# One group's sums of x made a stage earlier, two GpSimd sums put behind a quad, and the last rows stored in halves, in a fused windowed-attention and GEGLU kernel

## The chip, the cores and the metric

The kernel runs on one core of a Trainium2 chip. The core has five engines, each with its own queue of instructions: TensorE (PE in the profile; its weight loads are PEld), VectorE (DVE), ScalarE (ACT), GpSimd (POOL, here "Pool") and SyncE (SP), which here only issues transfers and passes semaphores on. The metric is the device time of one execution in microseconds, taken as the median of several runs.

## The reference

Eight batches of eight heads, 576 positions and head size 64 go through causal attention with a window of 128 and a linear (ALiBi) penalty; the result, 4608 tokens by 512, goes through a gated feed-forward block with an exact GELU.

```python
scores = scale * np.matmul(q, k.transpose(0, 1, 3, 2))
mask = (rel >= 0) & (rel < window)
scores = np.where(mask, scores + bias[None], -1000000000.0)
attn = np.exp(scores - max); attn = attn / (sum(attn) + 1e-09)
x = np.matmul(attn, v)             # as 4608 tokens x 512
...
g = x @ w_gate                     # 512 -> 1536
gelu = 0.5 * g * (1.0 + erf(g * inv_sqrt2))
return gelu * (x @ w_val) @ w_out  # 1536 -> 512
```

## The kernel before, in words

Attention works on batches of 576 tokens, the feed-forward block on nine groups (0 to 8) of 512 tokens. The attention result is kept transposed in `xT`, a ring of 2048 token columns. Group 7 holds tokens 3584 to 4095: its first 448 come from batch 6, its last 64 from batch 7, the last batch. The order of all instructions is written out by hand, and the work of a coming batch is put between the products of the running group. Each engine takes its own instructions strictly in order, so an instruction that waits holds up all behind it on that engine.

**Gate blocks.** `gate_val(g, f)` makes 128 of the 1536 hidden features: eight matmuls into two PSUM banks (L650), a GELU on ScalarE (L657) and the product of the two halves on VectorE into `hT` (L658). A group has twelve of them, f = 0 to 11. In groups 7 and 8, `gate_quad` makes f = 0 to 3 and f = 6 to 9 as two quads, each with seven block products in place of eight (L810). For that it needs sums and differences of parts of x (`combine_x`, VectorE, L785, kept in `T`) and of the gate and value weights (`combine_weights`, Pool, L768). A quad ends with products into `hT`: two on VectorE (L852), two on Pool (L853).

**Output products.** From group 2 on, the output projection is done in the same way: seven products P(1) to P(7) for each of two column halves a = 0 and 1, six matmuls of 256 columns each (L753). Their left sides need sums of parts of `hT`: `combine_left(g, lo, hi, which)` makes, for pairs lo to hi of feature blocks, s1 (which = 0), s2 (1), s4 (2) in `left` and the difference a21 (3) in place in `hT` (L728). Most are on VectorE; in groups 7 and 8 those of pairs 0 and 1, which come from the first quad, are on Pool. `gather_out` empties the PSUM banks: copies p1, u2, p5 and c21 on ScalarE (L866, L868, L872, L876), additions c11, c22 and c12 on VectorE (L870, L874, L879). Of a row block's two output tiles `hi` is finished by c21 and `lo` by c12; `finished` notes a store of 128 rows by 512 columns, which `store()` issues on SP (L677).

**Around the change.** In group 6 the output products of a = 0 are mixed with `values` of batch 7 (L504): products of probabilities and v into six PSUM banks, scaled by VectorE into `xT` (L579) with reciprocals that came by a transfer. P(1) of a = 1 uses the bank of the first of those six, so it waits until `scale[0]` and `scale[1]` have read it. Ahead of these two on VectorE stood c22 and then the four operations of `combine_x(g + 1, 0, 192)`. This call needs only tokens of batch 6; the rest, `combine_x(g + 1, 192, 256)`, needs batch 7 and stands at the group's end. On Pool, eight weight sums for the first quad are made in group 6 in two fours; a small copy to `mark` (L1270) ahead of each four holds Pool until the named VectorE result is there, and another mark (L1243) ahead of the second quad's sums waits for the last `combine_x`.

Of the kernel before, what the change touches and what calls it, by code (L numbers as in the profile page):

```python
# [36 lines left out]
def kernel(  # L37
# [10 lines left out]
    nc = tc.nc  # L48
    B, H, S, D = q.shape
# [4 lines left out]
    NG = NTOK // 512  # L54
# [618 lines left out]
    done, stores = [0], []  # L673
# [107 lines left out]
    def combine_x(g, lo=0, hi=256):  # L781
        b11, b12, b21, b22, t1, t2, t3, t4 = (t[:, :, lo:hi] for t in tokens(g) + sums_x(g))
        for to, a, b, op in ((t1, b12, b11, ALU.subtract), (t2, b22, t1, ALU.subtract),
                             (t3, b22, b12, ALU.subtract), (t4, b21, t2, ALU.subtract)):
            nc.vector.tensor_tensor(out=to, in0=a, in1=b, op=op)  # L785
# [66 lines left out]
            nc.vector.tensor_tensor(out=hidden(u, 0), in0=both(banks["x", u]), in1=both(gelus[u]), op=ALU.mult)  # L852
            nc.gpsimd.tensor_tensor(out=hidden(u, 1), in0=both(P5[u]), in1=both(gelus[2 + u]), op=ALU.mult)  # L853

    def finished(g, t, osb):
        r0 = 512 * g + 128 * t
        stores.append(dict(out=out[r0:r0 + 128, :], in_=osb))

    def gather_out(g, a, what, copy=nc.scalar.copy):
        x, y, z = (made.get((g, a, n)) for n in "xyz")  # L860
        if what == "p1":
            made[g, a, "lo"] = o_pool.tile([128, DM], FP32, name="osb")
            made[g, a, "hi"] = o_pool.tile([128, DM], FP32, name="osb")
        lo, hi = made[g, a, "lo"], made[g, a, "hi"]
        if what == "p1":
            copy(out=lo[:, 0:256], in_=x)  # L866
        elif what == "u2":
            copy(out=lo[:, 256:512], in_=x)  # L868
        elif what == "c11":
            nc.vector.tensor_tensor(out=lo[:, 0:256], in0=z, in1=lo[:, 0:256], op=ALU.add)  # L870
        elif what == "p5":
            copy(out=hi[:, 256:512], in_=y)  # L872
        elif what == "c22":
            nc.vector.tensor_tensor(out=hi[:, 256:512], in0=x, in1=hi[:, 256:512], op=ALU.add)  # L874
        elif what == "c21":
            copy(out=hi[:, 0:256], in_=x)  # L876
            finished(g, 2 + a, hi)
        elif what == "c12":
            nc.vector.tensor_tensor(out=lo[:, 256:512], in0=y, in1=lo[:, 256:512], op=ALU.add)  # L879
            finished(g, a, lo)  # L880

    def out_last(g):
        last = o_pool.tile([128, DM], FP32, name="osb")
# [233 lines left out]
    def out_products(g):  # L1117
        b = g + 2
        O = lambda what, a, copy=act: gather_out(g, a, what, copy)
        P = lambda n, a: product(g, n, a)  # L1120
        if b > B:
            for n, after in ((1, ("p1",)), (2, ()), (6, ("u2", "c11")), (5, ("p5",)), (7, ("c22",)), (4, ("c21",)),
                             (3, ("c12",))):
                for a in (0, 1):
                    P(n, a)
                    for what in after:
                        O(what, a)
                store()
                if n == 6 and g + 1 < NG:
                    combine_x(g + 1)  # L1130
            return
        P(1, 0)
        P(2, 0)
        O("p1", 0)
        urgent = 512 * (g + 2) - S * (b - 1)
        if b == B:
            P(6, 0)
            O("u2", 0)
            O("c11", 0)
            P(5, 0)  # L1140
            O("p5", 0)
            P(7, 0)
            O("c22", 0)
            combine_x(g + 1, 0, 192)
            scale = values(b - 1, later=True)
            P(4, 0)
            O("c21", 0)
            P(3, 0)
            scale[0]()
            scale[1]()  # L1150
            O("c12", 0)
            P(1, 1)
            O("p1", 1)
            store()
            P(2, 1)
            for do in scale[2:]:
                do()
            O("c11", 1)
            P(6, 1)
            O("u2", 1)  # L1160
            P(5, 1)
            O("p5", 1)
            P(7, 1)
            O("c22", 1)
            P(3, 1)
            O("c12", 1)
            P(4, 1)
            O("c21", 1)
            combine_x(g + 1, 192, 256)
            return  # L1170
        exp_table()
        O("c11", 0)
        later = []
        scores2(b, 0, later)
        A = later[0]
        P(6, 0)
        O("u2", 0, dve)
        P(5, 0)
        for n in (0, 1, 3):
            A[n]()  # L1180
        O("p5", 0)
        A[2]()
        P(7, 0)
        O("c22", 0)
        A[4]()
        for n in (5, 6, 7):
            A[n]()
        P(1, 1)
        P(4, 0)
        P(3, 0)  # L1190
        O("p1", 1)
        O("c21", 0)
        O("c12", 0)
        A[8]()
        A[9]()
        scores2(b, 2, later)
        A = later[1]
        P(2, 1)
        P(6, 1)
        O("u2", 1, dve)  # L1200
        O("c11", 1)
        add(b, 0, None, (0,))
        P(5, 1)
        for n in (0, 1, 3, 5):
            A[n]()
        O("p5", 1)
        A[2]()
        P(7, 1)
        O("c22", 1)
        A[4]()  # L1210
        for n in (6, 7):
            A[n]()
        store()
        scale, more = values(b - 1, urgent=urgent)
        for do in scale:
            do()
        P(4, 1)
        P(3, 1)
        O("c21", 1)
        for do in more:  # L1220
            do()
        O("c12", 1)
        A[8]()
        A[9]()
        add(b, 0, None, (2, 1))
        put_off.append(lambda: add(b, 2))
# [3 lines left out]
    for g in range(NG):  # L1230
# [7 lines left out]
        if g >= B - 1:  # L1238
            for f in range(NF):
                if f in QUADS:  # L1240
                    if g == B - 1 and f == 0:
                        sums = combine_weights(6)
                        nc.gpsimd.tensor_copy(out=mark, in_=sums_x(g)[3][0:1, 1, 254:256])  # L1243
                        for do in sums[:4]:
                            do()
                    gate_quad(g, f)
                    if g == B - 1 and f == 0:
                        for do in sums[4:]:
                            do()
                elif not any(f0 < f < f0 + 4 for f0 in QUADS):  # L1250
                    gate_val(g, f)
                if f == 4:
                    store()
                if f == 5:
                    combine_left(g, 0, 2, engine=nc.gpsimd)
                if f == 6:
                    combine_left(g, 2, 3, (0, 1))
            for which in ((0, 1), (3,), (2,)):
                for lo, hi in ((3, 5), (5, 6)) if 0 in which else ((2, 5), (5, 6)):
                    combine_left(g, lo, hi, which)  # L1260
            out_products(g)
            continue
        for f in range(9 if g == 0 else 0, NF):
            gate_val(g, f)
            if g == B - 2 and f in (2, NF - 1):
                if f == 2:
                    sums = combine_weights(0)
                else:
                    combine_left(g, 5, 6)
                nc.gpsimd.tensor_copy(out=mark, in_=hid[g][0:1, f, 510:512] if f == 2 else left[0:1, 2, 5, 0:2])  # L1270
                for do in (sums[:4] if f == 2 else sums[4:]):
                    do()
            if f == 1:
                for do in put_off:
                    do()
                put_off.clear()
                store()
            if g == 1 and f in (3, 5, 7, 9):
                combine_right(f // 2 - 1)
            if g in PRODUCTS and f in ((7, 9) if g == B - 2 else (7, 9, 11)):  # L1280
                combine_left(g, *{7: (0, 3), 9: (3, 5), 11: (5, 6)}[f])
            if g == 2 and f == 2:
                add(3, 2, act, (1,))
            if g == 0 and f == 10:
                masks_of_last_blocks(0, 8)
            if g == 0 and f == 9:
                for c in range(4):
                    for w in (0, 1):
                        transpose(1, w, c, (act, dve)[w])
            if 2 <= g < B - 1:  # L1290
                if f == (5 if g == 2 else 4):
                    sums4(g + 1)
                if f == (7 if g == 2 else 6):
                    gather(g + 1)
                if f == (9 if g == 2 else 8):
                    spread_dma(g + 1)
                if f == 9 and g + 2 < B:

                    nc.gpsimd.tensor_copy(out=mark, in_=hid[g][0:1, f, 0:2])  # L1299
                    if g + 3 < B:  # L1300
                        load_qk(g + 3)
                    load_v(g + 2)
# [47 lines left out]
```

## Time and profile before

| What | Value |
|---|---|
| median of 3 runs | 332.83 us (332.52 to 333.11) |
| the profiled execution: its own time | 334.23 us |
| its span, first to last instruction | 332.4 us |
| PE busy | 322.2 us, 97% |
| DVE busy | 257.0 us, 77% |
| ACT busy | 186.1 us, 56% |
| POOL busy | 145.8 us, 44% |
| granted TensorE clock | 1.0 over the span |

A row of a timeline has the start in microseconds of the span, the time from the start of the first to the end of the last instruction of the row, the engine, the line in the kernel, the operation, written tile, read tile, shapes and the number of instructions; in square brackets stands how long the engine was idle ahead of it and what ended that. A queue's own work (issuing a transfer) has a q behind the engine's name. A PE row with many matmuls lists starts and ends of a pipeline: one matmul of 256 columns takes about 0.27 us by itself and 0.11 us in a run of them.

### The profile page before, as it was taken

How to read it: one execution, taken by the hardware profiler on the slowest of the kernel's cores; microseconds unless marked ns; L12 is line 12 of the kernel's file. 1: busy time of each engine (PE TensorE's matmuls, PEld its weight loads, DVE VectorE, ACT ScalarE, POOL GpSimd, SP SyncE). 2: the span in 40 equal slices, each digit the busy share in tenths (PEclk: the TensorE clock that was granted, in tenths of full speed). 3: DMA queues.
4: the chain of work that ended last, by engine and by line, in shares of the span. 5: the costliest groups of instructions: out<-in, count | busy, mean ns of one | idle time of the engine just before them, and what ended most of it. 6: DMA issues, size and time to landing. Idle time of an engine off the chain costs nothing. (4 is left out here: it accounts for less than half of the span.)

```text
span 332.4 us, 9100 instructions
## 1 busy us (share of the span) xinstructions
PE 322.2 (97%) x3640; PEld 201.8 (61%) x3640; DVE 257.0 (77%) x529; ACT 186.1 (56%) x365; POOL 145.8 (44%) x179
## 2 busy tenths in 40 slices
PE   8999998999999999999999999999999899999995
PEld 6566654544554468445854585448644687788774
DVE  7788776365679967978798969976998876876692
ACT  7974686536798356434843384239533237636641
POOL 5974689280095085006900490032032528910720
PEclk9999999999999999999999999999999999999999
DMA  8999999999699999969994799559204230003003
GB/s 213 167 196 190 203 169 183 148 202 151 145 116 158 144 155 190 197 130 178 191 154 127 152 173 195 128 131 129 85 1 103 66 108 0 2 0 128 3 0 126
DMA packets 149630, 43.54 MB, mean 131 GB/s; under 512 B 133556, under 2 KB 142420, under 8 KB 149588
## 3 DMA queue, kind: packets, MB, share of 16 engines
q0 software_dynamic: 107456, 18.10, 72.4%
q1 hardware_dynamic: 38960, 18.69, 26.6%
q10 hardware_dynamic: 3172, 6.19, 8.2%
q8 instruction: 28, 0.46, 0.6%
q14 instruction: 14, 0.11, 0.1%
HBM read 43.65 MB, written 9.53 MB: 160 GB/s over the span
## 5 line engine op out<-in xcount | busy, mean ns | idle before, releaser
L657 ACT ACTIVATE gelu<-ps 128x512 bf16<-128x512 f32 (+3 forms) x101 | 55.9, 559 | 85.8 <-PE ps L650 78.2
L650 PE MATMUL ps<-xT,wg 128*128 128x512 bf16 (+4 forms) x408 | 96.4, 358 | 0.1
L650 PE MATMUL ps<-xT,wv 128*128 128x512 bf16 (+4 forms) x408 | 96.3, 358 | 0.0
L658 DVE TENSOR_TENSOR hT<-ps,gelu 128x512 bf16<-128x512 f32 (+3 forms) x101 | 62.0, 636 | 26.8 <-PE ps L650 19.0
L650 PEld LDWEIGHTS <-wv 128*128 128x128 bf16 x408 | 38.7, 98 | 41.2 <-DVE xT L558 0.5
L650 PEld LDWEIGHTS <-wg 128*128 128x128 bf16 x408 | 38.0, 98 | 38.7 <-issue 0.4
L234 ACT ACTIVATE P<-ps 128x512 bf16<-128x512 f32 (+1 forms) x108 | 52.4, 578 | 4.2 <-PE ps L303 2.1
L237 DVE TENSOR_TENSOR P<-P,emask 128x768 bf16<-128x768 bf16 x60 | 32.0, 554 | 8.1 <-ACT P L234 6.3
L753 PEld LDWEIGHTS <-hT 128*128 128x128 bf16 x336 | 31.8, 97 | 10.0 <-DVE xT L579 2.0
L117 POOL DMA_DIRECT2D vb<-in_v_dram x40 | 34.0, 893 | 3.9 <-DMA ks<-in_k_dram 1.2
L1299 POOL COPY mark<-hT 1x2 bf16<-1x2 bf16 x4 | 1.5, 366 | 74.1 <-DVE hT L658 74.1
L117 POOL DMA_DIRECT2D ks<-in_k_dram x30 | 25.4, 887 | 3.8 <-DMA qs<-in_q_dram 3.5
L753 PEld LDWEIGHTS <-left 128*128 128x128 bf16 x252 | 24.3, 98 | 3.0
L117 POOL DMA_DIRECT2D qs<-in_q_dram x30 | 25.1, 855 | 1.8 <-issue 0.9
L753 PE MATMUL ps<-wo,hT 128*128 128x256 bf16 x168 | 21.4, 273 | 2.8 <-DVE xT L579 1.7
L753 PE MATMUL ps<-right,hT 128*128 128x256 bf16 x168 | 22.1, 272 | 0.0
L753 PE MATMUL ps<-right,left 128*128 128x256 bf16 x168 | 20.3, 273 | 0.0
L504 PE MATMUL ps<-P,vb 64*64 64x192 bf16 (+2 forms) x752 | 18.3, 221 | 0.8 <-ACT P L234 0.7
L687 PE MATMUL ps<-wo,hT 128*128 128x512 bf16 x72 | 17.1, 380 | 1.1 <-issue 1.1
L853 POOL TENSOR_TENSOR hT<-qT,qs 128x512 bf16<-128x512 f32 x8 | 9.2, 1173 | 19.2 <-ACT qs L821 19.2
L504 PEld LDWEIGHTS <-vb 64*64 64x64 bf16 x752 | 15.0, 107 | 3.6 <-issue 2.7
L818 DVE TENSOR_TENSOR qT<-ps,qT 128x512 f32<-128x512 f32 x16 | 10.3, 686 | 8.5 <-PE ps L810 8.5
(141 smaller groups left out, 448.0 us busy)
## 6 DMA issues: line engine op xcount, KB each, us to landing
out_dram<-osb SPq DMA_DIRECT2D x36, 256.0 KB
rb<-rd ACTq DMA_DIRECT2D x10, 576.0 KB
vb<-in_v_dram POOLq DMA_DIRECT2D x32, 128.0 KB, 6.6
qs<-in_q_dram POOLq DMA_DIRECT2D x24, 128.0 KB, 5.8
ks<-in_k_dram POOLq DMA_DIRECT2D x24, 128.0 KB, 8.3
wo<-in_moe_w_out_dram POOLq DMA_DIRECT2D x4, 384.0 KB, 12.1
wg<-in_moe_w_gate_dram POOLq DMA_DIRECT2D x5, 256.0 KB, 8.4
wv<-in_moe_w_val_dram POOLq DMA_DIRECT2D x5, 256.0 KB, 8.9
```

The source lines that it names most:

```text
L117: nc.gpsimd.dma_start(out=t[at:at + n, j, :].rearrange("p (h d) -> p h d", h=H), in_=src[b][:, 128 * j:128 * j + n, :].rearrange("h p d -> ...
L234: nc.scalar.activation(out=dst, in_=src, func=AF.Exp, scale=0.125)
L237: nc.vector.tensor_tensor(out=dst, in0=dst, in1=m, op=ALU.mult)
L504: mm = nc.tensor.matmul(out=out, lhsT=lhsT, rhs=prob(b)[half, c, i, col:col + q1 - q0], start=all(t[2] != u for t in todo[:n]), stop=True, ...
L650: nc.tensor.matmul(out=ps[:, a:e], lhsT=w[:, c, 128 * f:128 * (f + 1)], rhs=xT[:, c, t0 + lo + a:t0 + lo + e], start=begins and a == 0, st ...
L657: nc.scalar.activation(out=gl[:, 0:n], in_=pg, func=AF.Gelu)
L658: nc.vector.tensor_tensor(out=hid[g][:, f, lo:hi], in0=pv, in1=gl[:, 0:n], op=ALU.mult)
L687: nc.tensor.matmul(out=acc[g], lhsT=hid[g][:, f, 128 * t:128 * (t + 1)], rhs=wo[:, f, :], start=(f == 0), stop=(f == NF - 1))
L753: nc.tensor.matmul(out=made[g, a, into], lhsT=lhsT, rhs=rhs, start=first and i == 0, stop=i == NF // 2 - 1, skip_group_check=True)
L818: nc.vector.tensor_tensor(out=to[u], in0=banks[n, u], in1=to[u], op=ALU.add)
L853: nc.gpsimd.tensor_tensor(out=hidden(u, 1), in0=both(P5[u]), in1=both(gelus[2 + u]), op=ALU.mult)
L1299: nc.gpsimd.tensor_copy(out=mark, in_=hid[g][0:1, f, 0:2])
```

## The change

Three edits, none of which changes an arithmetic operation.

1. `combine_x(g + 1, 0, 192)` leaves the output products of group 6 and is made in that group's gate blocks, behind block f = 6.
2. In groups 7 and 8, Pool makes only s1 and s2 of pairs 0 and 1 ahead of the second quad's products into `hT`; a21 and s4 of these pairs come behind them, a21 first.
3. In group 8 the `lo` tiles are stored in two halves of 256 columns: the first half once c11 has made it, the second behind c12. The second half of a = 1 is issued by ScalarE's queue, the rest by SP.

```diff
-    def finished(g, t, osb):
+    def finished(g, t, osb, cols=slice(0, 512), queue=None):
...
+        args = dict(out=out[r0:r0 + 128, cols], in_=osb[:, cols])
+        if queue is None:
+            stores.append(args)
+        else:
+            queue.dma_start(**args)
...
         elif what == "c11":
             nc.vector.tensor_tensor(out=lo[:, 0:256], in0=z, in1=lo[:, 0:256], op=ALU.add)
+            if g == NG - 1:
+                finished(g, a, lo, slice(0, 256))
...
-            finished(g, a, lo)
+            finished(g, a, lo, slice(256 if g == NG - 1 else 0, 512), nc.scalar if g == NG - 1 and a else None)
...
             O("c22", 0)
-            combine_x(g + 1, 0, 192)
             scale = values(b - 1, later=True)
...
                 if f == 5:
-                    combine_left(g, 0, 2, engine=nc.gpsimd)
+                    combine_left(g, 0, 2, (0, 1), engine=nc.gpsimd)
                 if f == 6:
                     combine_left(g, 2, 3, (0, 1))
+                    combine_left(g, 0, 2, (3, 2), engine=nc.gpsimd)
...
             gate_val(g, f)
+            if g == B - 2 and f == 6:
+                combine_x(g + 1, 0, 192)
```

VectorE's queue before, from the end of group 6's gate blocks into its output products; `osb` is an output tile, `T` holds the sums of x, `rb` the reciprocals:

```order
L728 TENSOR_TENSOR hT<-hT 128x256
L870 TENSOR_TENSOR osb<-ps,osb 128x256
L874 TENSOR_TENSOR osb<-ps,osb 128x256
L785 TENSOR_TENSOR T<-xT 128x2x192
L785 TENSOR_TENSOR T<-xT,T 128x2x192
L785 TENSOR_TENSOR T<-xT 128x2x192
L785 TENSOR_TENSOR T<-xT,T 128x2x192
L579 TENSOR_TENSOR xT<-ps,rb 128x64
L579 TENSOR_TENSOR xT<-ps,rb 128x448
L879 TENSOR_TENSOR osb<-ps,osb 128x256
```

The four L785 rows stand between c22 (L874) and the first two scalings. The same place with the change, where the lines of `gather_out` have moved to L874, L880 and L885:

```order
L728 TENSOR_TENSOR hT<-hT 128x256
L874 TENSOR_TENSOR osb<-ps,osb 128x256
L880 TENSOR_TENSOR osb<-ps,osb 128x256
L579 TENSOR_TENSOR xT<-ps,rb 128x64
L579 TENSOR_TENSOR xT<-ps,rb 128x448
L885 TENSOR_TENSOR osb<-ps,osb 128x256
```

The scalings now follow c22 directly. VectorE's queue with the change in group 6's gate blocks, from the reciprocals of batch 7 on; the first L658 row is blocks 5 and 6, the second is block 7:

```order
L445 RECIPROCAL r<-ps 128x160
L658 TENSOR_TENSOR hT<-ps,gelu 128x512 x2
L785 TENSOR_TENSOR T<-xT 128x2x192
L785 TENSOR_TENSOR T<-xT,T 128x2x192
L785 TENSOR_TENSOR T<-xT 128x2x192
L785 TENSOR_TENSOR T<-xT,T 128x2x192
L658 TENSOR_TENSOR hT<-ps,gelu 128x512
L728 TENSOR_TENSOR left<-hT 128x768
```

The four sums now stand between the products of blocks 6 and 7, which before stood together.

Pool's queue before, from the second half of the weight sums for group 7's second quad to the first quad of group 8; `hT<-qT_100,qs_95` are a quad's products into `hT`:

```order
L768 TENSOR_TENSOR emask<-wg,P_105 128x512 x2
L728 TENSOR_TENSOR left<-hT 128x512
L728 TENSOR_TENSOR left<-left,hT 128x512
L728 TENSOR_TENSOR left<-hT,left 128x512
L728 TENSOR_TENSOR hT<-hT 128x2x256
L853 TENSOR_TENSOR hT<-qT_100,qs_95 128x2x256 x4
```

and with the change:

```order
L768 TENSOR_TENSOR emask<-wg,P_105 128x512 x2
L728 TENSOR_TENSOR left<-hT 128x512
L728 TENSOR_TENSOR left<-left,hT 128x512
L853 TENSOR_TENSOR hT<-qT_100,qs_95 128x2x256 x2
L728 TENSOR_TENSOR hT<-hT 128x2x256
L728 TENSOR_TENSOR left<-hT,left 128x512
L853 TENSOR_TENSOR hT<-qT_100,qs_95 128x2x256 x2
```

Two of the four sums (s4 and a21) have gone behind the second quad's two products, in the order a21, s4; the last row of each listing holds group 8's first-quad products (before, the four of both quads are in one row). The same is done in group 8.

More of the change, by code (lines that the diff above doesn't have):

```diff
@@ L853, in gate_quad @@
             nc.gpsimd.tensor_tensor(out=hidden(u, 1), in0=both(P5[u]), in1=both(gelus[2 + u]), op=ALU.mult)
-    def finished(g, t, osb):
+    def finished(g, t, osb, cols=slice(0, 512), queue=None):
         r0 = 512 * g + 128 * t
-        stores.append(dict(out=out[r0:r0 + 128, :], in_=osb))
+        args = dict(out=out[r0:r0 + 128, cols], in_=osb[:, cols])
[3 more added lines that the diff above has]
+            queue.dma_start(**args)
     def gather_out(g, a, what, copy=nc.scalar.copy):
```

## The prediction

> **What bounds the kernel now.** I read the page's busy times first (PE is the engine that is nearly always busy), then the chain that ended last, then the timeline around the two places where that chain leaves PE. Here is the chain from the profile of before: start, length, engine and line.
>
> ```profile
> 290.67 0.69 DVE hT L658
> ...
> 291.40 8.88 PE ps L753 x79
> ...
> 328.70 0.42 DVE osb L879
> ```
>
> From 266.5 us to the end the chain is PE (the dropped pieces are PE, or waits of 0.12 us and less), but for one VectorE product at 290.67 and the last addition. So after 266 us time is won only where PE stands, and behind its last matmul. The timeline at the first place, group 6:
>
> ```profile
> 261.82 1.60 PE L504 MATMUL ps<-P,vb 64*64 64x192 bf16 x88
> 261.98 0.42 DVE L874 TENSOR_TENSOR osb<-ps,osb 128x256 f32<-128x256 f32 x1 [1.05 <-ACT osb L872]
> 262.33 0.75 DVE L785 TENSOR_TENSOR T<-xT 128x384 bf16<-128x384 bf16 x1
> ...
> 264.02 0.82 PE L753 MATMUL ps<-wo,left 128*128 128x256 bf16 x6
> ...
> 264.23 1.30 DVE L785 TENSOR_TENSOR T<-xT 128x384 bf16<-128x384 bf16 x1
> ...
> 265.45 0.35 DVE L785 TENSOR_TENSOR T<-xT,T 128x384 bf16<-128x384 bf16 x1
> 265.72 0.74 DVE L579 TENSOR_TENSOR xT<-ps,rb 128x64 bf16<-128x64 f32 x2
> ...
> 266.52 1.49 PE L753 MATMUL ps<-wo,hT 128*128 128x256 bf16 x12 [1.69 <-DVE xT L579]
> ```
>
> PE starts P(3) of a = 0, six matmuls, at 264.02 and P(1) of a = 1 only at 266.52. A run of them goes at 0.109 us each (24 from 319.25 to 321.87, rows below), so P(1) was due at 264.02 + 6 x 0.109 = 264.68: PE lost 1.84 us. P(1) waits for the two scalings of 265.72, which stand in VectorE's queue behind four L785 sums, begun at 262.33 right after c22 (261.98) and over at 265.80. The rows show no idle time ahead of any of them: it is the order of the queue that holds P(1).
>
> **Edit 1, where it takes from.** Without the four sums the scalings follow c22 at 262.40. The data they read come from the matmuls of 261.82, all done by 263.42, so the two scalings (0.74) end by 264.16 at the latest, 0.5 ahead of 264.68. The 1.84 us go. What is late next is the rest of VectorE's queue up to c22 of a = 1:
>
> ```profile
> 266.72 2.46 DVE L579 TENSOR_TENSOR xT<-ps,rb 128x64 bf16<-128x64 f32 x8
> ...
> 269.10 0.41 DVE L870 TENSOR_TENSOR osb<-ps,osb 128x256 f32<-128x256 f32 x1
> ...
> 270.06 0.42 DVE L874 TENSOR_TENSOR osb<-ps,osb 128x256 f32<-128x256 f32 x1 [0.56 <-ACT osb L872]
> ```
>
> Eight scalings and c11 take 269.10 - 266.72 = 2.38 and then 0.41. With the change they can start only behind c12, which needs P(3): about 264.9 + 0.34, so c11 runs from 267.6 to 268.0, and c22, wanted at 270.06 - 1.84 = 268.22, is not late, by 0.2 us. From there PE, ScalarE, VectorE and Pool keep their distances: the last sums of x, Pool's mark behind them and its weight sums all follow PE, so group 7's first quad starts 1.84 earlier.
>
> **Edit 1, where it puts.** The four sums go behind the product of block 6. From the timeline of before:
>
> ```profile
> 248.75 2.26 POOL L768 TENSOR_TENSOR P<-P,wg 128x512 bf16<-128x512 bf16 x2
> ...
> 250.09 0.69 DVE L658 TENSOR_TENSOR hT<-ps,gelu 128x512 bf16<-128x512 f32 x1 [0.23 <-PE ps L650]
> ...
> 251.82 0.69 DVE L658 TENSOR_TENSOR hT<-ps,gelu 128x512 bf16<-128x512 f32 x1 [1.03 <-PE ps L650]
> ...
> 252.75 1.29 ACTq L459 DMA_DIRECT2D rb<-rd  x2
> ...
> 257.59 0.68 DVE L658 TENSOR_TENSOR hT<-ps,gelu 128x512 bf16<-128x512 f32 x1
> ...
> 258.45 1.47 PE L753 MATMUL ps<-wo,hT 128*128 128x256 bf16 x12
> 258.72 0.69 DVE L658 TENSOR_TENSOR hT<-ps,gelu 128x512 bf16<-128x512 f32 x1 [0.45 <-PE ps L650]
> ...
> 260.46 0.18 POOL L1270 COPY mark<-left 1x2 bf16<-1x2 bf16 x1 [9.46 <-DVE left L728]
> ```
>
> That product ends at 250.78, the next began at 251.82 after 1.03 idle. Pool's two weight sums last until 251.01, so they can hold the first new sum for 0.23; the others take 0.27 to 0.38 each (0.35 in the row of 265.45; the same kind of sum took 1.30 at 264.23, with Pool at work). The four end near 252.2, and block 7's product comes 0.3 to 0.5 late. That hands itself down to block 10's product (257.59), which ends by 258.8 instead of 258.27; PE first needs it for the sixth matmul of P(1), at 258.45 + 5 x 0.109 = 259.0, its weights 0.1 sooner. Block 11's product had 0.45 idle and absorbs the rest. Cost 0; without that margin up to 0.3. Edit 1 together: 1.84, between 1.4 and 1.85.
>
> **Edit 2.** Group 7, end of the second quad, then the same place in group 8 with the end of group 7's products ahead of it:
>
> ```profile
> 287.16 1.16 POOL L728 TENSOR_TENSOR left<-hT,left 128x512 bf16<-128x512 bf16 x1
> ...
> 289.39 2.37 POOL L853 TENSOR_TENSOR hT<-qT,qs 128x512 bf16<-128x512 f32 x2
> ...
> 289.62 1.13 DVE L728 TENSOR_TENSOR left<-left,hT 128x256 bf16<-128x256 bf16 x1
> ...
> 290.33 0.71 PE L753 MATMUL ps<-wo,hT 128*128 128x256 bf16 x5
> ...
> 291.87 0.41 DVE L728 TENSOR_TENSOR left<-hT 128x512 bf16<-128x512 bf16 x1
> ```
>
> ```profile
> 296.32 0.42 DVE L785 TENSOR_TENSOR T<-xT,T 128x512 bf16<-128x512 bf16 x1
> 297.02 0.42 DVE L874 TENSOR_TENSOR osb<-ps,osb 128x256 f32<-128x256 f32 x1 [0.28 <-ACT osb L872]
> ...
> 316.51 2.32 POOL L853 TENSOR_TENSOR hT<-qT,qs 128x512 bf16<-128x512 f32 x2 [2.41 <-ACT qs L821]
> ...
> 317.48 0.34 DVE L728 TENSOR_TENSOR left<-hT 128x256 bf16<-128x256 bf16 x1
> ...
> 317.85 1.13 DVE L728 TENSOR_TENSOR left<-left,hT 128x256 bf16<-128x256 bf16 x1
> ...
> 319.25 2.78 PE L753 MATMUL ps<-wo,hT 128*128 128x256 bf16 x24
> ...
> 320.13 0.42 DVE L728 TENSOR_TENSOR left<-hT 128x512 bf16<-128x512 bf16 x1
> ...
> 321.24 0.29 DVE L728 TENSOR_TENSOR left<-left,hT 128x256 bf16<-128x256 bf16 x1
> ...
> 321.87 2.78 PE L753 MATMUL ps<-right,left 128*128 128x256 bf16 x24
> ```
>
> In group 7, P(1) starts at 290.33 but goes on with its sixth matmul at 291.40 (chain, above) instead of 290.33 + 5 x 0.109 = 290.87: 0.53 lost. It waits for block 10's product, queued on VectorE behind two sums that Pool held up: the one of 289.62 ended 0.17 behind the first half of Pool's row of 289.39 (1.13 us against 0.29 for the same sum at 321.24). In group 8, exactly 28.92 later, Pool had no weight sums to make, its products began at 316.51, and P(1) ran without a gap. With the change Pool's products in group 7 come at the same point: its first two sums are over when the third (s4) starts at 287.16, and the products are due at 316.51 - 28.92 = 287.59. So the 0.53 goes.
>
> What comes in its place: Pool now has two sums of 1.16 (row of 287.16) behind the products, from 318.83 to about 321.1 in group 8. The VectorE sum of 320.13 has both inputs in SBUF, as the held ones had, and would end near 321.4 instead of 320.55. The last s2 (321.24) then ends near 322.36 instead of 321.53; PE wants it for the sixth matmul of P(6), at 321.87 + 0.55 = 322.4, its weights 0.1 sooner: about 0.1 lost. The same 0.1 in group 7, and more behind it: VectorE's chain there, which ran from 291.87 through the sums of 296.32 to c22 at 297.02 with hardly a pause, ends its first sum at 292.46 (Pool's end at 321.1 - 28.92 = 292.18, and 0.28 for a sum of this length) against 292.28. The sums of x left room for c22 from about 296.66, since neighbouring rows overlap by 0.08; now it can't begin before 296.84, where 297.02 - 0.53 = 296.49 would be wanted, and P(4) waits for c22. Group 7 so keeps about 0.18 of its 0.53, and group 8 loses 0.1. Edit 2 together: 0.08 won. Bounds: 0.53 won if no sum meets Pool's; 0.35 lost if the chain of both groups is later by a quarter microsecond than worked out.
>
> **Edit 3.** The last store is issued on SP behind c12 and its data follow; one window after it, and a transfer that ScalarE issued (row of 252.75 above) with the windows where its data begin (columns: window, its length, busy time per engine, clock, DMA share, GB/s):
>
> ```profile
> 329.15 0.33 SPq L677 DMA_DIRECT2D out_dram<-osb  x1
> ```
>
> ```profile
> 253.00:254.00 1.00, 1.00 (x7) 0.47 (x5) 0.96 (x2) 0.20 (x1) 0.00 (x0) 1.00 0.00 0
> 254.00:255.00 1.00, 1.00 (x7) 0.41 (x5) 1.00 (x3) 0.60 (x1) 0.00 (x0) 1.00 0.78 200
> ...
> 330.00:331.00 1.00, 0.00 (x0) 0.00 (x0) 0.00 (x0) 0.00 (x0) 0.00 (x0) 1.00 0.74 281
> ```
>
> At 381 KB per microsecond (281 in 0.74) a store of 262 KB takes 0.69, so data end at 330.74 and begin 0.9 behind the issue. Half the bytes take 0.34: 0.35 won. But ScalarE's queue issues it: its transfer of 252.75 had no data until about 254.22, 1.47 behind the issue, 0.57 more than SP's, though of another form. The end therefore moves between 0.35 earlier and 0.25 later, and the value lies nearer to SP's row for its form (rows of 128 partitions): 0.15 won. The Trainium skill, "DMA: Bandwidth & Descriptors", section Specifications, gives one first-byte latency of about 0.6 us for the sync and the scalar path alike; by that rule the edit would win 0.35 and the whole sum be 2.27. The rows of 252.75 and 329.15 speak against the equal footing. The first halves go out behind c11, ahead of the other stores of this group, and cost nothing.
>
> **Sum.** 1.84 + 0.08 + 0.15 = 2.07 us from the profiled execution, whose span of 332.4 becomes 330.3 and its own time of 334.23, 1.8 more than the span, 332.2. The median of the runs shown, 332.83, lies 1.4 below that execution; taken from it, the same 2.07 gives 330.8 us. A measurement of this kernel can tell about 0.2%, 0.67 us, from no change.
>
> **Rivals.** (a) *Edit 2 keeps its whole 0.53*, because VectorE's sum of the later pairs slips in between Pool's two: 330.8 - 0.45 = 330.3. Against it: 320.13 falls into Pool's second sum (about 319.9 to 321.1). The Trainium skill, "SBUF — State Buffer", section Who interferes with whom, says that of a VectorE instruction with two SBUF inputs and a GpSimd one the earlier issued blocks the other; by this it takes VectorE to be 0.25 us earlier. The trace agrees where it has such pairs (1.13 against 0.29). Chance 0.15.
>
> (b) *Group 6 takes part of it back*: VectorE leaves the gate blocks later than worked out, by one further Pool sum (1.1), so that P(1) and P(6) of a = 0 wait and c22 of a = 1 has lost its 0.2 us: 0.7 given back, 331.5. For it: the margins of 0.2 are small. Chance 0.10.
>
> (c) *The wait isn't the queue's*: something else that was ready at the same time, such as the reciprocals' transfer, holds the scalings to 265.7. Then only edits 2 and 3 are left, 332.6. Against it: four sums and scalings follow each other without idle time, and that transfer was issued at 252.75, 13 us ahead. Chance 0.05.
>
> (d) *Slower*: each of the four sums in block 6 waits out a whole Pool sum, as those of 262.33 to 265.80 did in part. At 1.3 each they take 5.2 instead of 1.4, so they end at 256.0, block 7's product comes 4.2 late, and block 10's ends 3.4 behind what PE can bear: PE stands that long in place of 1.84, and 330.8 + 3.4 = 334.2. It decides once the four sums end behind about 254.6 instead of 252.2. Against it: Pool's weight sums end at 251.01 and its mark holds it until 260.46. Chance 0.03.
>
> **How the numbers follow.** The forecast has 0.67: 330.8. Its own bounds reach from 332.83 - (1.85 + 0.53 + 0.35) = 330.1 to 332.83 - (1.4 - 0.35 - 0.25) = 332.0; all bad ends together are unlikely, and the range 330.1 to 331.6 takes in (a) and (b). Faster by over 0.2%: forecast, (a) and (b), 0.92. Within 0.2%: (c), 0.05. Slower: (d), 0.03.
>
> **What would show it.** Right: in group 6 no gap between P(3) and the next P(1), scalings directly behind c22, four L785 sums of about 1.4 us in all near 250.8, and all of group 7 some 1.8 earlier against group 6's gate blocks; in groups 7 and 8 a VectorE sum of about 1.2 us behind block 11 and a short gap in P(6); in group 7 c22 directly behind the sums of x; at the end a last issue on ScalarE and 3.1 us or so from the last addition to the end of the span, against 3.28. Wrong: a gap of PE in group 6 ahead of P(1) or P(6) of a = 0, a P(4) of group 7 that waits by more than 0.4, or a tail longer than before.

## The result and the profile after

The changed kernel takes 330.51 us in the median of 6 runs (329.86 to 331.56), the kernel before, in runs beside it, 332.88 us (6 runs, 332.52 to 333.21). The ratio is 0.9931, with a 95% interval of 0.9914 to 0.9948: faster by 2.4 us. The profiled execution has a time of 331.56 and a span of 329.8, against 334.23 and 332.4.

The chain that ended last, from the profile of after:

```profile
285.01 3.45 PE ps L650 x16
288.46 6.59 PE ps L753 x60
295.28 2.78 PE ps L753 x24
...
317.19 9.29 PE ps L753 x84
```

The VectorE product of group 7 (290.67 in the profile before) is gone from the chain. A new break stands at 295.28: the piece before it ends at 295.05. Now the first place, group 6, in the timeline of after:

```profile
261.65 1.60 PE L504 MATMUL ps<-P,vb 64*64 64x192 bf16 x88
261.81 0.42 DVE L880 TENSOR_TENSOR osb<-ps,osb 128x256 f32<-128x256 f32 x1 [1.05 <-ACT osb L878]
...
262.87 0.76 DVE L579 TENSOR_TENSOR xT<-ps,rb 128x64 bf16<-128x64 f32 x2 [0.63 <-PE ps L504]
...
263.85 0.82 PE L753 MATMUL ps<-wo,left 128*128 128x256 bf16 x6
...
264.50 1.47 PE L753 MATMUL ps<-wo,hT 128*128 128x256 bf16 x12
```

P(3) starts at 263.85 and P(1) of a = 1 at 264.50, 0.65 later: six matmuls at 0.109, and no idle time in brackets. The scalings come directly behind c22 (L880) and now wait 0.63 for their data. Where the four sums of x have gone, in the same timeline, VectorE and Pool:

```profile
248.58 2.26 POOL L768 TENSOR_TENSOR P<-P,wg 128x512 bf16<-128x512 bf16 x2
...
249.92 0.69 DVE L658 TENSOR_TENSOR hT<-ps,gelu 128x512 bf16<-128x512 f32 x1 [0.22 <-PE ps L650]
250.53 0.53 DVE L785 TENSOR_TENSOR T<-xT 128x384 bf16<-128x384 bf16 x1
...
251.64 0.35 DVE L785 TENSOR_TENSOR T<-xT,T 128x384 bf16<-128x384 bf16 x1
252.00 0.69 DVE L658 TENSOR_TENSOR hT<-ps,gelu 128x512 bf16<-128x512 f32 x1
...
258.55 0.69 DVE L658 TENSOR_TENSOR hT<-ps,gelu 128x512 bf16<-128x512 f32 x1 [0.23 <-PE ps L650]
```

The first sum is held until Pool's second weight sum has ended at 250.84, so it takes 0.53 instead of 0.35. All four are done at 251.99. The last block's product (258.55) still waits for PE, by 0.23, so VectorE has caught up by then.

Group 7 at the end of its second quad and in its output products:

```profile
285.56 2.32 POOL L853 TENSOR_TENSOR hT<-qT,qs 128x512 bf16<-128x512 f32 x2 [0.48 <-ACT qs L821]
...
288.30 2.78 PE L753 MATMUL ps<-wo,hT 128*128 128x256 bf16 x24
289.00 1.15 POOL L728 TENSOR_TENSOR left<-hT,left 128x512 bf16<-128x512 bf16 x1
...
289.18 1.26 DVE L728 TENSOR_TENSOR left<-hT 128x512 bf16<-128x512 bf16 x1
...
290.92 2.81 PE L753 MATMUL ps<-right,left 128*128 128x256 bf16 x24
...
294.48 0.42 DVE L785 TENSOR_TENSOR T<-xT,T 128x512 bf16<-128x512 bf16 x1
294.81 0.75 DVE L880 TENSOR_TENSOR osb<-ps,osb 128x256 f32<-128x256 f32 x2
295.28 1.47 PE L753 MATMUL ps<-right,hT 128*128 128x256 bf16 x12 [0.24 <-DVE osb L880]
```

Pool's products now wait for their input (0.48) instead of coming late. P(1) and the products behind it run as 24 matmuls without a gap; the next 24, with P(6), take 2.81 instead of 2.78, which is the short gap there. Behind block 11 a VectorE sum takes 1.26 beside Pool's s4 (0.42 for the later sums of this length), and two c22 additions stand one behind the other at 294.81, directly behind the sums of x. That is the break in the chain: P(4) at 295.28 waits for c22.

The end, with ScalarE's queue issuing the last store, and the two windows behind it (columns as in the prediction):

```profile
326.51 0.42 DVE L885 TENSOR_TENSOR osb<-ps,osb 128x256 f32<-128x256 f32 x1 [0.23 <-PE ps L753]
326.96 0.37 ACTq L861 DMA_DIRECT2D out_dram<-osb  x1
```

```profile
327.00:328.00 1.00, 0.00 (x0) 0.00 (x0) 0.00 (x0) 0.00 (x0) 0.00 (x0) 1.00 0.69 237
328.00:329.00 1.00, 0.00 (x0) 0.00 (x0) 0.00 (x0) 0.00 (x0) 0.00 (x0) 1.00 0.25 83
```

Data still move in both windows. From the last addition's end (326.93) to the span's end (329.78) it is 2.85 us, against 3.29 (329.12 to 332.41) before.

**A measure that takes the scatter out.** Executions of one kernel differ by a microsecond or more. The thirteen profiles show where: ahead of group 3's output products. Their P(1) starts here in before, in after, and in the experiment with the sums behind block 5 (further down), one row from each:

```profile
154.80 1.47 PE L753 MATMUL ps<-wo,hT 128*128 128x256 bf16 x12
```

```profile
154.64 1.47 PE L753 MATMUL ps<-wo,hT 128*128 128x256 bf16 x12
```

```profile
152.86 1.47 PE L753 MATMUL ps<-wo,hT 128*128 128x256 bf16 x12
```

In all thirteen profiles this start lies between 152.7 and 156.3, with no order by kernel. From it to P(1) of group 6 all thirteen take 103.64 to 103.66. So the experiments are read by stretches, worked out from the starts of single matmuls in each trace, in us. The stretches are A: group 6's P(1) to group 7's first quad; B: group 7's P(1) to group 8's first quad; C: group 8's P(1) to the start of the last matmul; T: last addition's end to the span's end (not the tile `T`); R: group 3's P(1) to the span's end. The two stretches from a first quad to the P(1) behind it are 19.13 in every run.

| Kernel | A | B | C | T | R | median | ratio to before, 95% |
|---|---|---|---|---|---|---|---|
| before | 12.74 | 9.79 | 9.138 | 3.291 | 177.62 | 332.88 | |
| after | 10.88 | 9.60 | 9.167 | 2.846 | 175.14 | 330.51 | 0.9931 (0.9914 to 0.9948) |
| edit 1 alone | 10.88 | 9.79 | 9.138 | 3.283 | 175.73 | 331.07 | 0.9943 (0.9923 to 0.9963) |
| edit 2 alone | 12.74 | 9.60 | 9.164 | 3.284 | 177.43 | 332.69 | 0.9984 (0.9964 to 1.0005) |
| edit 3 alone | 12.74 | 9.81 | 9.139 | 2.845 | 177.18 | 332.79 | 0.9986 (0.9970 to 1.0002) |
| before, Pool later | 10.88 | 9.80 | 9.138 | 3.282 | 175.76 | 331.58 | 0.9948 (0.9930 to 0.9967) |
| after, c22 first | 10.88 | 9.27 | 9.164 | 2.830 | 174.79 | 330.32 | 0.9900 (0.9881 to 0.9919) |
| after, last store on SP | 10.88 | 9.59 | 9.153 | 2.787 | 175.07 | 330.74 | 0.9909 (0.9885 to 0.9932) |
| after, block 8 | 11.28 | 9.59 | 9.160 | 2.828 | 175.51 | 331.38 | 0.9932 (0.9908 to 0.9955) |
| after, block 5 | 10.88 | 9.59 | 9.164 | 2.833 | 175.12 | 330.03 | 0.9896 (0.9876 to 0.9915) |
| after, whole rows on ScalarE | 10.88 | 9.60 | 9.165 | 3.303 | 175.59 | 331.58 | 0.9937 (0.9914 to 0.9959) |
| after, c22 first and last store on SP | 10.88 | 9.28 | 9.163 | 2.775 | 174.74 | 330.21 | 0.9898 (0.9868 to 0.9929) |
| after once more | 10.88 | 9.60 | 9.166 | 2.842 | 175.13 | 330.83 | 0.9916 (0.9886 to 0.9947) |

R falls by 2.48 with the change: 1.86 in A, 0.19 in B, -0.03 in C, 0.45 in T, together 2.46 before rounding; the other 0.02 lie mostly between group 3's and group 6's P(1), where nothing was changed. The same kernel run again comes to 175.13 against 175.14.

### The profile page after: what moved, and what is told of

Its sections match the earlier page's. It is cut to its first block, busy times and chain, and to the rows that moved or that the text cites. A ratio compares the mean times of both kernels' runs of the same rounds, so it can differ in the third digit from the quotient of the medians.

```text
span 329.8 us, 9103 instructions
## 1 busy us (share of the span) xinstructions
PE 321.9 (98%) x3640; PEld 201.3 (61%) x3640; DVE 255.0 (77%) x529; ACT 186.2 (56%) x365; POOL 145.6 (44%) x179
## 4 chain that ended last, share of the span: by engine, by line
PE 83%; DMA 11%; ACT 2%; POOL 1%; issue 1%; DVE 0%; ACTq 0%; DVEq 0%
PE ps L650 43%; PE ps L753 19%; PE ps L810 7%; PE ps L687 5%; PE ps L504 4%; DMA wo<-in_moe_w_out_dram 4%; PE ps L303 2%; DMA wv<-in_moe_w_val_dram 2%; DMA vb<-in_v_dram 2%; ACT P L234 1%; DMA rd<-r 1%; DMA wo<-in_q_dram 1%; PE ps L440 1%; PE ps L221 1%; PE ps L707 1%
## 5 line engine op out<-in xcount | busy, mean ns | idle before, releaser
L658 DVE TENSOR_TENSOR hT<-ps,gelu 128x512 bf16<-128x512 f32 (+3 forms) x101 | 61.9, 636 | 25.4 <-PE ps L650 19.0
```

Of the source, the lines that this page charges most:

```text
L658: nc.vector.tensor_tensor(out=hid[g][:, f, lo:hi], in0=pv, in1=gl[:, 0:n], op=ALU.mult)
```

## The experiments

The first four and the last three ran on one chip (the kernel before beside them 333.24, 29 runs, and 333.34, 17 runs), the four between on another (333.69, 7 runs). Each ratio is to the kernel before on the same chip.

**Edit 1 alone.** The kernel before with

```diff
-            combine_x(g + 1, 0, 192)
...
+            if g == B - 2 and f == 6:
+                combine_x(g + 1, 0, 192)
```

> The kernel before with edit 1 alone: the four sums of x behind gate block 6 of group 6. If VectorE's order was the wait, PE's gap ahead of P(1) of a = 1 (1.85 us over the pace of a run) is gone and nothing takes its place: 1.85 us less, 331.0. If something else held the scalings (rival c), the gap stays and the time with it, 332.9. If the gate blocks pay for it (rival b), a new gap of 0.3 us or more stands at P(1) or P(6) of a = 0: 331.3 to 331.7.

A falls by 1.86 and nothing else moves (R by 1.89). Edit 1 gives three quarters of the gain.

**Edit 2 alone.** The kernel before with

```diff
-                    combine_left(g, 0, 2, engine=nc.gpsimd)
+                    combine_left(g, 0, 2, (0, 1), engine=nc.gpsimd)
...
+                    combine_left(g, 0, 2, (3, 2), engine=nc.gpsimd)
```

> The kernel before with edit 2 alone: Pool's a21 and s4 behind the second quad's products in groups 7 and 8. If VectorE's later sums meet Pool's two and c22 of group 7 is then late behind the sums of x, the gap of 0.53 us in P(1) of group 7 goes and a wait of some 0.33 us more than before stands ahead of P(4); group 8 loses 0.03: 0.16 us less, 332.7, within the noise. If the 0.53 is kept (rival a), 332.35.

B falls by 0.19 and C grows by 0.03, together 0.17 against the 0.16 expected; R falls by 0.19, 0.01 of it ahead of group 6, where nothing was changed. By the medians alone, whose interval takes in 1, it couldn't be told from nothing.

**Edit 3 alone.** The kernel before with the half stores of the diff above, the last on ScalarE's queue.

> The kernel before with edit 3 alone: the last rows stored in halves, the last half on ScalarE's queue. If the tail is the last store's bytes and the waits behind it, the time from the last addition's end to the end of the span falls from 3.29 to 2.88 us and the total by 0.41, to 332.5. If ScalarE's queue is as slow to begin as its broadcasts were (0.57 us more than SP), the tail grows by 0.2 us.

T falls by 0.45 and R by 0.44. Here too the interval of the medians takes in 1; it is T that shows the gain.

**Pool's second four weight sums later.** Edit 1 takes the sums of x out from ahead of the scalings, and it also takes them out from beside Pool's weight sums. Here only the second is done: VectorE's order is that of the kernel before, but Pool makes the second four weight sums of group 6 once the sums of x are there.

```diff
             combine_x(g + 1, 0, 192)
+            nc.gpsimd.tensor_copy(out=mark, in_=sums_x(g + 1)[3][0:1, 1, 190:192])
+            for do in sums[4:]:
+                do()
...
-                nc.gpsimd.tensor_copy(out=mark, in_=hid[g][0:1, f, 510:512] if f == 2 else left[0:1, 2, 5, 0:2])
-                for do in (sums[:4] if f == 2 else sums[4:]):
-                    do()
+                if f == 2:
+                    nc.gpsimd.tensor_copy(out=mark, in_=hid[g][0:1, f, 510:512])
+                    for do in sums[:4]:
+                        do()
```

> The kernel before, none of the three edits; only Pool's second four weight sums in group 6 wait for the four sums of x instead of running beside them. If the sums of x were long because Pool held them (3.5 us for 1.3 us of work), they now end near 263.7, the scalings near 264.4, and P(1) of a = 1 starts with a gap under 0.1 us: 1.8 us less, 331.1, as with edit 1. If it was their place in the queue alone that cost the time, the gap stays at 1.8 us: 332.9.

In the kernel before, Pool's second four weight sums ran from 260.60 to 265.31, beside the sums of x:

```profile
260.60 2.26 POOL L768 TENSOR_TENSOR P<-wg,wv 128x512 bf16<-128x512 bf16 x2
262.82 2.49 POOL L768 TENSOR_TENSOR emask<-wg,P 128x512 bf16<-128x512 bf16 x2
```

The timeline of this kernel in group 6:

```profile
261.27 0.42 DVE L874 TENSOR_TENSOR osb<-ps,osb 128x256 f32<-128x256 f32 x1 [1.05 <-ACT osb L872]
261.61 0.35 DVE L785 TENSOR_TENSOR T<-xT 128x384 bf16<-128x384 bf16 x1
...
262.54 0.35 DVE L785 TENSOR_TENSOR T<-xT,T 128x384 bf16<-128x384 bf16 x1
...
262.80 0.75 DVE L579 TENSOR_TENSOR xT<-ps,rb 128x64 bf16<-128x64 f32 x2
262.95 0.17 POOL L1145 COPY mark<-T 1x2 bf16<-1x2 bf16 x1 [12.68 <-DVE T L785]
263.09 2.25 POOL L768 TENSOR_TENSOR P<-wg,wv 128x512 bf16<-128x512 bf16 x2
...
263.95 1.47 PE L753 MATMUL ps<-wo,hT 128*128 128x256 bf16 x12
```

The four sums still stand ahead of the scalings, but take 1.28 (261.61 to 262.89) instead of 3.47 (262.33 to 265.80), and P(1) comes without a stop: A is 10.88, all of edit 1's gain, by another edit. So the place in the queue alone doesn't cost 1.84. It costs it because Pool's sums ran at the same time and held VectorE's. Free of Pool, the sums would have been over in time where they stood: 262.33 + 1.28 + 0.74 = 264.35 for the scalings, ahead of the 264.68 at which P(1) was due. Pool's later start hurt nothing here; VectorE's eight scalings beside it read PSUM and `rb` and kept their 2.46 us.

**The sums behind block 8, and behind block 5.** How much room does the new place need?

```diff
-            if g == B - 2 and f == 6:
+            if g == B - 2 and f == 8:
```

> The changed kernel, but group 7's sums of x are made behind gate block 8 of group 6 instead of behind block 6. Theory 1 (block 6 leaves the sums their room; behind block 8 the 1.4 us of VectorE push block 10's product by about 1.15 beyond where it stands, of which 0.6 is slack at the products that read it): TensorE stops for about 0.5 us within group 6's output products, so P(1) to group 7's quad takes about 11.4 instead of 10.9 and the time is about 331.0. Theory 2 (anywhere ahead of the output products is as good): 10.88 and 330.5.

```profile
257.59 0.71 PE L753 MATMUL ps<-wo,hT 128*128 128x256 bf16 x5
257.78 1.28 DVE L658 TENSOR_TENSOR hT<-ps,gelu 128x512 bf16<-128x512 f32 x2
258.52 0.69 PEld L753 LDWEIGHTS <-hT 128*128 128x128 bf16 x7 [0.50 <-DVE hT L658]
```

P(1) stops behind five matmuls for block 10's product, and A is 11.28: 0.40 of edit 1's 1.86 is lost, near the 0.5 expected. So the gain of edit 1 does hang on the place, and block 6 has the room.

```diff
-            if g == B - 2 and f == 6:
+            if g == B - 2 and f == 5:
```

> The changed kernel, but the sums are made behind gate block 5 of group 6. Pool's first four weight sums of that group run there. Theory 1 (Pool's operations hold VectorE's additions while both run, as the four sums of x took 3.5 us in the kernel before for 1.5 us alone): the sums take 2 us or more here instead of 1.46, block 7's product ends about 0.7 later, and TensorE loses 0.1 to 0.25 at the end of group 6's gate blocks; the time is 330.6 to 330.8. Theory 2 (Pool and VectorE do not hinder one another much): 1.46 for the sums, no loss, 330.5.

```profile
246.79 2.40 POOL L768 TENSOR_TENSOR P<-P,wg 128x512 bf16<-128x512 bf16 x2
...
247.83 0.34 DVE L785 TENSOR_TENSOR T<-xT 128x384 bf16<-128x384 bf16 x1
...
248.21 1.19 DVE L785 TENSOR_TENSOR T<-xT,T 128x384 bf16<-128x384 bf16 x1
...
249.33 0.35 DVE L785 TENSOR_TENSOR T<-xT 128x384 bf16<-128x384 bf16 x1
```

Half of the first theory held: the four sums take 2.11 us (247.83 to 249.94) instead of 1.46, since the second is held until Pool ends at 249.19. The other half failed: A is 10.88 and R 175.12, so no time is lost. Block 10's product is still there for P(1)'s sixth matmul. The median of 330.03 is no gain either: R is the same, and this profile's group 3 starts 1.8 earlier than that of after.

**c22 first.** If the stop ahead of P(4) in group 7 is VectorE's order, the sums of x need only go one place further back:

```diff
-                if n == 6 and g + 1 < NG:
+                if n == 7 and g + 1 < NG:
                     combine_x(g + 1)
```

> The changed kernel, but in group 7's output products the sums of x of group 8 come behind both c22 additions instead of ahead of them. Theory 1 (VectorE's order makes P(4) late: in the changed kernel's trace c22 stands directly behind the sums of x and TensorE stops 0.52 us ahead of P(4), against 0.19 before): the stop goes back to 0.19, the stretch from group 7's P(1) to group 8's first quad goes from 9.60 to about 9.27, the time falls by 0.33 to about 330.2 against the 330.5 of the changed kernel. Theory 2 (the sums, started later, make the scalings of group 8 late, as they did in group 6 of the kernel before): the stop moves from P(4) to the last weights or the first quad, the stretch stays at 9.6 or grows to 10 or more, and the time is 330.5 or more.

```profile
293.12 0.42 DVE L880 TENSOR_TENSOR osb<-ps,osb 128x256 f32<-128x256 f32 x1 [1.05 <-ACT osb L878]
293.78 0.42 DVE L880 TENSOR_TENSOR osb<-ps,osb 128x256 f32<-128x256 f32 x1 [0.23 <-PE ps L753]
294.12 0.41 DVE L785 TENSOR_TENSOR T<-xT 128x512 bf16<-128x512 bf16 x1
```

```profile
292.21 2.86 PE L753 MATMUL ps<-right,hT 128*128 128x256 bf16 x24
```

c22 now waits for ScalarE (1.05) and PE (0.23), where in after P(4) waited for c22. From the matmul ahead of it to P(4) it is 0.19 again (0.52 in after, 0.11 in a run of matmuls), B is 9.27, and R 174.79: 0.35 less than after. The first theory held to the hundredth, and the first quad of group 8 isn't late for the sums.

**The last store on SP, and whole rows on ScalarE.** Edit 3 changes the size of the last store and its queue. These two runs change one each, against after:

```diff
-            finished(g, a, lo, slice(256 if g == NG - 1 else 0, 512), nc.scalar if g == NG - 1 and a else None)
+            finished(g, a, lo, slice(256 if g == NG - 1 else 0, 512), None)
```

> The changed kernel, but the last half of the last group's rows is issued by SyncE like all the others, not by ScalarE. From the last addition's end to the span's end the changed kernel takes 2.846 us, the kernel before 3.291. Theory 1 (the gain of the half stores is the smaller last transfer, and the queue matters little: ScalarE's issue took 0.372 with first data 0.96 behind its start, SyncE's issues 0.333 with 0.83 to 0.90): 2.75 to 2.85 here, so the time is the same or shorter by up to 0.1. Theory 2 (SyncE is still at the issue of the half before, so the last issue stands behind it there): about 0.3 us longer, 3.1 to 3.2, and the time longer by 0.3.

```diff
-            if g == NG - 1:
-                finished(g, a, lo, slice(0, 256))
...
-            finished(g, a, lo, slice(256 if g == NG - 1 else 0, 512), nc.scalar if g == NG - 1 and a else None)
+            finished(g, a, lo, slice(0, 512), nc.scalar if g == NG - 1 and a else None)
```

> The changed kernel, but the last group's lower rows are stored whole again (128 rows of 2048 bytes, as before the change), the last of them still issued by ScalarE. From the last addition's end to the span's end: 3.291 in the kernel before (whole rows, SyncE), 2.83 to 2.85 in the changed kernel (halves, ScalarE), 2.79 with halves on SyncE. Theory 1 (the size of the last transfer makes the whole gain of the third edit, the queue is worth 0.06 at most): 3.2 to 3.35. Theory 2 (the queues that the stores stand on make a good part of it, since SyncE's own last waits got shorter as well): 2.9 to 3.1.

T in the four: whole rows 3.29 on SP and 3.30 on ScalarE, halves 2.79 on SP and 2.83 to 2.85 on ScalarE. The queue is worth 0.01 to 0.06, the halves 0.46 to 0.50: the first theory in both runs. One number in the expectation for the store on SP was too high: by the packet records the first data of ScalarE's store in after come 0.88 behind the issue's start, not 0.96, and so within SP's 0.83 to 0.90. The records of the transfers and of SyncE's waits split T (us behind the last addition's end, last column the rest to the span's end):

```
                          data all stored   SyncE's waits over   then to the span's end
before  (whole, SP)             1.74               2.43                 0.86
whole on ScalarE                1.77               2.44                 0.87
after   (halves, ScalarE)       1.43               1.98                 0.87
halves on SP                    1.38               1.92                 0.87
```

Halving takes 0.34 to 0.36 off the data and a further 0.12 to 0.15 off the waits behind them. At the end SyncE makes ten waits one after the other, at a distance of about 0.06 us where the semaphore is already there. In before the sixth is over 2.15 behind the last addition, once the last store has landed, and four more follow until 2.39; in after the eighth is over at 1.82 and two more follow until 1.94. So it is in all thirteen profiles: four waits behind the last store's with whole rows, two with halves, that is with two stores more. Why two more stores move the last one's wait two places back is not shown.

**Both.** After with c22 first and the last store on SP, and after once more beside it.

> The changed kernel with the sums of x of group 8 behind both c22 additions of group 7's output products, and the last half store on SyncE. The two touch different places, so the stretch from group 7's P(1) to group 8's first quad should be 9.27 (9.60 in the changed kernel) and the tail from the last addition 2.79 (2.83 to 2.85): 0.37 less than the changed kernel on the same chip, 0.33 of it from the order of the sums. If instead the two single gains do not add, the stretch is longer than 9.3 or the tail longer than 2.85.

> The changed kernel once more, beside the two others on one chip: group 6's P(1) to the quad 10.88, group 7's P(1) to the quad 9.60, tail 2.83 to 2.85, and a time 2.3 to 2.6 below the kernel before. Single runs differ by up to 1.5 because of the first 150 us; if the edits have any share in that, the start of group 6's P(1) would differ between the kernels' medians, else only as much as between runs of one kernel.

B 9.28, T 2.775, R 174.74: the gains add, 0.39 less than after (175.13). The median is 330.21 against 330.83. It is the fastest of the kernels by R, by 2.88 ahead of the kernel before. Group 3's start is 154.19 in after once more and 154.64 in after. Two profiles of one kernel don't settle whether the edits have a part in that start, but the times do: taking R from the span of every execution (an estimate, as R was measured in one) puts the median start at 153.1 to 154.3 for all kernels, while the twelve executions of edit 1 alone reach from 152.6 to 156.4. No part of the edits is visible in it.

## Why the prediction was right, and where its terms were off

The forecast was 2.07 us, made of 1.84 + 0.08 + 0.15. R shows 2.48, made of 1.86 + 0.16 + 0.45. The sign, the largest term and its mechanism were right; of the 0.4 that is missing, 0.30 is edit 3.

**Edit 1, 1.84 against 1.86.** The scalings follow c22, P(1) has no stop, c22 of a = 1 is not late, and all that follows comes earlier by the same amount. The four sums end at 251.99, where 252.2 was worked out, and PE has no gap in P(1) or P(6). One sentence of the step was too simple: "it is the order of the queue that holds P(1)". The run with Pool later keeps that order and has no stop. Order and Pool's hold were needed together; of the 3.47 us that the sums took, 2.2 were waiting for Pool. The prediction had the row that says so (1.30 for a sum that took 0.35 without Pool), but used it only for the price of the new place. It would have shown a second way to the same gain.

**Edit 2, 0.08 against 0.16.** The step ran as worked out: P(1)'s 0.53 goes, a VectorE sum of 1.26 appears behind block 11, c22 slides directly behind the sums of x, and P(4) waits. That wait is at the edge of a sign of being wrong ("a P(4) of group 7 that waits by more than 0.4"): PE is idle for 0.24 in the row and P(4) starts 0.41 behind the pace of a run, of which before had 0.08; the loss is the forecast one. "Group 7 so keeps about 0.18 of its 0.53" came out at 0.19. Off was "group 8 loses 0.1": it lost 0.03. Put on after's clock, the last s2 was forecast to end at 322.36 - 2.22 = 320.14 and ended at 320.16; what was mis-sized is how soon PE wants it. The forecast wanted it 0.1 ahead of the sixth matmul of P(6); that matmul starts at 320.22, 0.06 behind the sum and 0.02 behind the pace of a run. Rival (a), in which VectorE's sum slips in between Pool's two, did not come true here (1.26), though in the run with block 5 one sum of x (247.83, 0.34) did just that, and Pool's two then took 2.40 instead of 2.26. The Trainium skill, "SBUF — State Buffer", section Who interferes with whom, has both: the two contend, and the order of issue decides which one is blocked. The runs agree (0.34 and 2.40 there, 1.26 here).

**Edit 3, 0.15 against 0.45.** This is the term that failed; its bounds (0.35 earlier to 0.25 later) did not hold it either. Two things were wrong in the step "The end therefore moves between 0.35 earlier and 0.25 later". First, ScalarE's queue was charged with up to 0.57 from the transfer of `rb`, a transfer of another form. In after, data of the ScalarE store begin 0.88 behind the issue's start, those of the stores on SP 0.83 to 0.90, and the two runs put the queue at 0.01 to 0.06. The Trainium skill, "DMA: Bandwidth & Descriptors", section Specifications, treats both paths alike: the runs agree with that and not with the row chosen, while its figure of about 0.6 us is lower than the 0.83 to 0.90 seen here. Second, the sum stopped at the end of the data. It left out SyncE's waits behind them, of which 0.12 went as well.

**The rivals.** (b) and (d) did not happen: no wait in P(1) or P(6) of group 6, and only one of the four sums was held, by 0.18. The run with block 8 shows that VectorE leaving the gate blocks late, as in (b), does cost PE time (0.40), but only two blocks further on. (c) is refuted by the kernels whose A is shorter by 1.86, one of them with the sums still ahead of the scalings.

**The time.** 2.07 taken from 332.83 gave 330.8; 330.51 was measured. That the median moved by 2.37 and R by 2.48 is no contradiction, as group 3's start alone scatters by more than that difference.

## What to carry to other kernels

A slow group of instructions ahead of a late one has two cures: move the group, or take away what makes it slow; compare its rows with the same instructions elsewhere in the trace before choosing. When a stall goes, look at once for what is late next and whether its order can be swapped too: here 0.35 us more lay one place further back. For a store at the very end, price the bytes and the waits behind it, and take a latency only from a transfer of the same form.

## What the runs showed of the hardware that was not expected

- All scatter visible in the thirteen profiles arises in the first 153 to 156 us. From group 3's P(1) on, stretches repeat to 0.01 to 0.02 us, so one profile resolves an edit of 0.03 us that a median of 12 runs cannot.
- A held VectorE sum of two SBUF inputs ends 0.2 to 0.3 behind the end of the Pool operation that held it (249.40 against 249.19; 290.44 against 290.15). It waits for one Pool operation, not for all that are queued: in the kernel before, the first sum of x (262.33) ended at 263.08, 0.22 behind the Pool operation that ended at 262.86, while Pool's next two went on until 265.31.
- Packets of 1024 bytes took 46 ns and those of 2048 bytes 85 ns, so halving a row's length took about 8% off the rate.
- SyncE's last waits take about 0.06 us each even where the semaphore is already set, one behind the other, on the path to the end.
